# Long convolution on TensorE: whole-array outer stages, 64x64 quarters in the middle, and a new order of the work

## The chip, the core and the metric

The kernel runs on one core of one Trainium2 chip. The metric is the device time of one execution in microseconds. The median of three runs before the change is 393.52 us (393.09 to 393.66).

## The reference

Two layers are computed side by side, both on a sequence of S = 2048 with D = 1024 channels in bf16, and their outputs are concatenated.

Layer A is a long convolution. A filter of four taps is run over `k`, the result is multiplied by `v` to give `kv`, and `kv` is convolved along the sequence with `ssm_k` (one filter of length 2048 for each channel), in the reference by an FFT of length 4096. A skip term is added and the result is multiplied by `q`:

```
kv  = k_shift * v
y_f = rfft(pad(kv)) * rfft(pad(ssm_k))
y   = irfft(y_f)[:S] + kv * ssm_D
a   = q * y
```

Layer B is a diagonal state-space recurrence with 1024 complex states:

```
for t in range(L):
    h = Lam_bar * h + Bu[:, t, :]
y = 2 * real(einsum(h, Cmat)) + x * Dskip
```

## The kernel before

The convolution is a discrete Fourier transform of length 4096 split into two stages of 128 and 32 points, done with matmuls against constant matrices. It has these steps. The name in front is the task's name in the code.

- `kvm`, `kva`, `kvb`, `kvc` (DVE) make `kv` for one residue n2 of the time index modulo 16 (16 residues).
- `hl`, `hT`, `hc` load the filter and transpose it on TensorE (L571), because its time index lies along the free dimension.
- `am` (L548, for `kv`) and `hm` (L590, for the filter) are stage 1: matmuls with 64 rows, one for each half p of the partitions. `ae` and `he` copy the result from PSUM on ACT, `ast` and `hst` store it to DRAM (`Ys_kv`, `Ys_h`), with 2 KB or 1 KB rows.
- `lh`, `lk` load it back regrouped, for pair i of 16 pairs of frequency groups; `lw` loads the pair's constants into one of three slots.
- `sh`, `sk` (L616) are stage 2 for the filter and for `kv`: matmuls with 64 output columns, two of them for one PSUM bank. `she`, `ske` (L624) copy on ACT.
- `pr` (L630) multiplies on DVE all four combinations of real and imaginary half (4096 elements per partition).
- `sa` (L640) is the inverse of stage 2: four matmuls of 64 rows for each output, which add the four products with their signs. `sae` (L647) copies, `vst` stores to DRAM (`Vs`).
- `vl` loads again, `a3` (L668) is the inverse of stage 1 with 64 output columns, `a3e` copies, `qm` multiplies by `q`, `ost` stores.

Layer B goes over 16 chunks of 128 time steps: `U` (L441, 128-column matmuls), `ue` (ACT), `r1`, `r2`, `sc` (the scan), `r3`, `r4` (all DVE), `y` (L485, 512-column matmuls, with the skip term in L490), `ye` (ACT), `yst`. `cy` carries the state from chunk to chunk.

All tasks are written by hand into one long text, `ORDER`, which names every task, its place in SBUF (`a` with a unit number) and its PSUM banks (`p`). Each engine executes its instructions in that order. Loads are issued on the queue of SP, stores on the queue of POOL. An engine that waits holds up all that stands behind it on the same engine.

The change and the steps of the prediction touch `a_constants`, `ORDER` and the tasks `kp`, `vp`, `am`, `hT`, `hm`, `l2`, `s2`, `s2e`, `pr`, `sa`, `sae`, `vl`, `qp`, `a3_`, `ost`.

Of the kernel before, what the change touches and what calls it, by code (L numbers as in the profile page):

```python
# [31 lines left out]
def a_constants():
    n1 = np.arange(64)[:, None]; k1 = np.arange(64)[None, :]
    ang = 2 * np.pi * n1 * (k1 + 0.5) / N1
    F1 = np.concatenate([np.cos(ang), -np.sin(ang)], axis=1)
    F1 = np.concatenate([F1, F1], axis=0)
    G = np.concatenate([np.cos(ang.T), -np.sin(ang.T)], axis=0) * 2 / NFFT
    n2 = np.arange(N2); k2 = np.arange(N2)
    W = np.zeros((128, NPAIR, 640))
    for g in range(NG):  # L40
        i, gs = divmod(g, 2)
        fw = np.zeros((N2, 2, 2, 2, 2, N2))
        wr = np.zeros((2, N2, N2, 2, 2))
        wi = np.zeros((2, N2, N2, 2, 2))
        for l in range(2):
            kk = (32 * l + g) + N1 * k2
            phi = 2 * np.pi * np.outer(n2, kk + 0.5) / NFFT
            cph, sph = np.cos(phi), np.sin(phi)
            fw[:, 0, l, 0, l, :] = cph
            fw[:, 1, l, 0, l, :] = sph  # L50
            fw[:, 0, l, 1, l, :] = -sph
            fw[:, 1, l, 1, l, :] = cph
            wr[l, :, :, 0, l] = cph.T
            wr[l, :, :, 1, l] = sph.T
            wi[l, :, :, 0, l] = -sph.T
            wi[l, :, :, 1, l] = cph.T
        W[:, i, gs * 128:(gs + 1) * 128] = fw.reshape(128, 128)
        rows = slice(64 * gs, 64 * gs + 64)
        W[rows, i, 256:384] = wr.reshape(64, 128)
        W[rows, i, 384:512] = -wr.reshape(64, 128)  # L60
        W[rows, i, 512:640] = wi.reshape(64, 128)
# [9 lines left out]
kvm.1:a36 bT.4.1:p2 bcv.7.1 bT.0.1:p1 bcv.0.1 bc.7.0 bl.4.0:a26 bT.4.0:p5 bT.2.1:p4 bcv.2.1 cl.1.0:a27 cT.1.0:p7 cc.1.0 x.1:a52 bl.1.0:a34
U.1.0.0:a32p0 bT.1.0:p1 bc.1.0 U.1.1.0:p4 U.1.1.1 U.1.3.0:p3 U.1.3.1 bc.4.0 ue.1.1 kva.1 hl.2:a40 bl.5.0:a35 ue.1.3 vp.1.0:a42 stt x.0:a44 z2 z1
U.0.0.0:a46p6 kvb.1:a45 kp.-2.0 U.0.0.1 ue.0.0 bT.5.0:p7 U.0.3.0:p1 U.0.3.1 ue.0.3 U.0.1.0:p5 kp.-2.1 kvm.0:a48 cl.3.1:a29 vp.0.0:a30 bc.5.0 U.0.1.1
vp.0.1 kvc.1 bcv.4.1 cT.3.1:p4 kva.0 cc.3.1 cl.0.0:a28 kp.1.0 am.1.1:p3p2 ae.1.0.1:a34 U.1.0.1 ue.1.0 ae.1.1.1 kp.1.1 U.0.2.0:p6 U.0.2.1 kvm.2:a4
ue.0.2 ue.0.1 x.2:a16 U.2.0.0:a18p1 kvb.0:a17 kva.2 am.1.0:p7p4 ae.1.1.0 ae.1.0.0 cT.0.0:p3 kvc.0 am.0.0:p0p2 am.0.1:p6p5 ae.0.0.1:a26 ast.1 kvb.2:a45
U.1.2.0:p4 ld_sd:a17 ae.0.1.0 hl.0:a36 ae.0.1.1 hl.3:a38 hl.1:a24 hT.0.6:p7 hc.0.6:a20 kvm.3:a48 U.2.0.1 ae.0.0.0 hm.0.6.1:p6p2 he.0.6.1.0:a22
U.2.1.0:p5 he.0.6.1.1 r1.0:a28 hm.0.6.0:p7p0 he.0.6.0.0 he.0.6.0.1 hT.0.1:p6 ue.2.0 cl.2.0:a21 hst.0.6.1 vp.1.1 kvc.2 kva.3 am.2.0:p2p7 cx.6.1 r2.0:h0
ae.2.0.0:a46 cl.1.1:a4 cT.1.1:p0 cc.0.0 U.2.1.1 ue.2.1 kvb.3:a20 cc.1.1 cl.2.1:a5 cl.3.0:a6 kp.2.0 ae.2.1.0 cT.2.1:p1 am.2.1:p2p3 sc.0.1 ae.2.1.1
# [12 lines left out]
hT.1.1:p1 hc.1.1:a42 hst.0.3.0 hst.0.7.1 y.1.1.2 y.1.1.3 vp.4.0:a26 ye.1.0:a43 hc.1.4:a52 ue.3.3 r1.3:a36 ast.4 U.4.1.1 hm.1.1.1:p5p1 he.1.1.1.1:a18
kp.5.0 he.1.1.1.0 hm.1.1.0:p4p2 kvb.7:a42 vp.3.0:a40 vp.3.1 y.2.0.0:p6 ye.1.1 yst.1 ue.4.1 y.2.0.1 hT.1.7:p1 y.2.0.2 he.1.1.0.1 kvc.6 hc.1.7:a34
hm.1.5.0:p5p3 hm.1.5.1:p0p2 he.1.5.1.0:a22 he.1.5.1.1 kp.4.0 he.1.5.0.0 y.2.1.0:p1 kp.4.1 he.1.5.0.1 y.2.1.1 kvc.7 vp.4.1 am.7.0:p0p2 ae.7.0.0:a46
am.7.1:p5p3 kvm.8:a28 ae.7.1.1 ae.7.1.0 kva.8 he.1.1.0.0 kvb.8:a35 ae.7.0.1 hc.1.2:a25 y.2.0.3 y.2.1.2 r2.3:h0 ye.2.0:a40 cy.3 U.4.3.0:p0 kvc.8
U.4.3.1 ue.4.3 y.2.1.3 sc.3.0 am.8.1:p3p2 ye.2.1 yst.2 am.8.0:p4p5 hm.1.2.1:p7p6 hst.1.1.0 hT.1.0:p0 sc.3.1 ast.7 ae.8.1.1:a42 he.1.2.1.1:a28
hT.1.6:p1 hc.1.0:a16 hd.1 hT.1.3:p2 he.1.2.1.0 hm.1.2.0:p6p0 he.1.2.0.0 hst.1.2.0 yst.0 U.4.2.0:p7 hc.1.3:a35 he.1.2.0.1 ae.8.0.1 kp.5.1 hst.1.2.1
U.4.2.1 hm.1.0.1:p6p2 kvm.11:a36 kp.6.0 x.5:a41 U.5.0.0:a6p0 ue.4.2 U.5.0.1 U.5.2.0:p3 ae.8.0.0 he.1.0.1.1:a30 U.5.2.1 lw.1:w1 hc.1.6:a25 he.1.0.1.0
ae.8.1.0 r1.4:a48 hm.0.5.1:p7p4 ue.5.0 he.0.5.1.0:a32 kva.11 hm.1.0.0:p2p1 hm.0.5.0:p6p5 ast.8 hst.1.1.1 he.0.5.0.1 he.1.0.0.0 he.0.5.0.0 he.0.5.1.1
# [645 lines left out]
```

## Time and profile before

| | |
|---|---|
| median of the runs | 393.52 us |
| the profiled execution's own time | 393.14 us |
| its span, first to last instruction | 390.9 us |
| mean granted TensorE clock | 0.988 |
| DMA | 92.41 MB, mean 236 GB/s |
| stage 1 of the convolution (L548, L590) | 37.8 to 183.0 us |
| stage 2 and its inverse (L616, L640) | 182.1 to 319.2 us |
| inverse of stage 1 (L668) | 348.1 to 370.7 us |

The profile is one execution, recorded by the hardware. PE is TensorE's matmuls, PEld its weight loads, DVE VectorE, ACT ScalarE, POOL GpSimd, SP SyncE, which here only issues DMAs. "Busy" is the time in which an engine had an instruction running. In the strip of 40 digits each digit is the busy share of one fortieth of the span in tenths. A shape such as 128\*64 beside a matmul is that of the weights: rows by columns. Matmuls are pipelined: an isolated one lasts some 0.38 us, while in a stream of 512-column ones the next starts after 0.216 us, so costs are taken from the distance between starts.

### The profile page before, as it was taken

What the parts mean: (1) busy time and instruction counts of PE and PEld (TensorE: products, weight loads), DVE (VectorE), ACT (ScalarE), POOL (GpSimd) and SP (SyncE); (2) the same over time, 40 slices, a digit from 0 to 9 for tenths busy, and PEclk for the clock granted to TensorE, in tenths of its full rate; (3) what the DMA queues carried; (4) which work ended last, traced back from release to release, by engine and by line L of the source; (5) the groups of instructions that cost most, each with busy time, mean ns of one, the idle gap of its engine ahead of it and who ended that gap; (6) DMA issues with size and microseconds to landing.
All of it is one profiled execution on the core that took longest, in us unless ns stands there. A gap on an engine that the chain in (4) does not pass through costs nothing.

```text
span 390.9 us, 9198 instructions
## 1 busy us (share of the span) xinstructions
PE 363.6 (93%) x3821; PEld 236.1 (60%) x3849; DVE 320.8 (82%) x257; ACT 277.9 (71%) x530; POOL 67.8 (17%) x111
## 2 busy tenths in 40 slices
PE   4689799999999999999999999996999999999990
PEld 2589689456658577567554547553564549955440
DVE  5768998899989999999999925959369398998950
ACT  4698599985699956628677999795588973158530
POOL 5000112035004430311000020010002011001171
PEclk9999999999999999999999999999999999999996
DMA  6999999999948979677757787699586728998695
GB/s 189 263 272 210 277 282 204 259 314 341 260 110 219 266 242 223 203 242 244 256 203 223 250 284 217 164 202 352 149 231 216 227 121 283 297 245 229 237 267 183
DMA packets 55365, 92.41 MB, mean 236 GB/s; under 512 B 29422, under 2 KB 31502, under 8 KB 55324
## 3 DMA queue, kind: packets, MB, share of 16 engines
q1 hardware_dynamic: 45468, 58.21, 58.4%
q0 software_dynamic: 9856, 33.62, 25.6%
q8 instruction: 30, 0.49, 0.6%
q14 instruction: 11, 0.09, 0.1%
HBM read 51.96 MB, written 33.55 MB: 219 GB/s over the span
## 4 chain that ended last, share of the span: by engine, by line
PE 68%; DMA 12%; ACT 7%; issue 6%; SPq 3%; POOL 1%; DVE 0%; POOLq 0%; ACTq 0%
PE bank L441 24%; PE bank L485 22%; PE bank L616 7%; DMA arena<-in_A_k_dram 6%; PE bank L640 6%; PE bank L571 4%; DMA arena<-in_A_ssm_k_dram 3%; PE bank L590 2%; DMA wslot<-a_c_W 2%; PE bank L548 2%; ACT arena L647 2%; PE bank L490 2%; DMA out_dram<-arena 1%; ACT arena L624 1%; ACT arena L675 1%
## 5 line engine op out<-in xcount | busy, mean ns | idle before, releaser
L485 PE MATMUL bank<-CT,gslot 128*128 128x512 bf16 x484 | 122.3, 381 | 2.2 <-issue 0.9
L441 PEld LDWEIGHTS <-BT 128*128 128x128 bf16 x2048 | 115.7, 98 | 11.9 <-issue 9.4
L441 PE MATMUL bank<-arena,BT 128*128 128x128 bf16 x2048 | 121.9, 219 | 0.2
L485 PEld LDWEIGHTS <-gslot 128*128 128x128 bf16 x512 | 44.1, 98 | 53.2 <-issue 12.7
L469 DVE TENSOR_TENSOR_SCAN gslot<-rtab,gslot 128x1040 bf16<-128x1040 f32 x32 | 72.8, 2311 | 3.6 <-ACT gslot L465 3.1
L624 ACT CAST arena<-bank 128x512 bf16<-128x512 f32 x128 | 67.1, 657 | 10.2 <-PE bank L616 10.1
L630 DVE TENSOR_TENSOR arena<-arena 128x4096 bf16<-128x4096 bf16 x16 | 36.3, 2289 | 30.9 <-ACT arena L624 30.4
L443 ACT CAST arena<-bank 128x512 bf16<-128x512 f32 x64 | 38.7, 618 | 28.4 <-PE bank L441 20.7
L496 ACT CAST arena<-bank 128x512 bf16<-128x512 f32 x32 | 19.4, 606 | 38.3 <-PE bank L485 35.2
L456 DVE TENSOR_TENSOR arena<-arena,Z 128x4096 bf16<-128x4096 bf16 x16 | 36.6, 2287 | 7.5 <-ACT arena L443 3.4
L554 ACT CAST arena<-bank 128x512 bf16<-128x512 f32 x64 | 35.3, 617 | 6.5 <-PE bank L548 6.2
L596 ACT CAST arena<-bank 128x512 bf16<-128x512 f32 x64 | 35.4, 632 | 3.7 <-PE bank L590 3.5
L456 DVE TENSOR_TENSOR arena<-gslot,Z 128x4096 bf16<-128x4096 bf16 x16 | 36.6, 2288 | 0.6
L647 ACT CAST arena<-bank 128x512 bf16<-128x512 f32 x64 | 34.7, 641 | 2.5 <-PE bank L640 2.5
L616 PE MATMUL bank<-arena,wslot 128*64 128x512 bf16 x256 | 32.4, 389 | 3.4 <-DMA wslot<-a_c_W 3.4
L525 DVE TENSOR_TENSOR arena<-arena 128x4096 bf16<-128x4096 bf16 (+3 forms) x16 | 30.0, 1881 | 4.5 <-ACT arena L335 3.2
L599 POOL DMA_DIRECT2D Ys_h<-arena x32 | 23.2, 725 | 38.3 <-ACT arena L596 38.2
L640 PE MATMUL bank<-arena,wslot 64*128 64x512 bf16 x256 | 29.6, 377 | 0.0
L490 PE MATMUL bank<-Dd,arena 128*128 128x128 bf16 x128 | 28.2, 220 | 0.3 <-issue 0.2
L650 POOL DMA_DIRECT2D Vs<-arena x16 | 8.5, 535 | 112.0 <-ACT arena L647 76.5
L557 POOL DMA_DIRECT2D Ys_kv<-arena x16 | 11.6, 727 | 85.7 <-ACT arena L554 83.1
L616 PEld LDWEIGHTS <-wslot 128*64 128x64 bf16 x256 | 13.8, 110 | 19.4 <-issue 5.0
(95 smaller groups left out, 353.9 us busy)
## 6 DMA issues: line engine op xcount, KB each, us to landing
Ys_kv<-arena POOLq DMA_DIRECT2D x16, 512.0 KB, 4.7
Ys_h<-arena POOLq DMA_DIRECT2D x32, 256.0 KB, 3.9
out_dram<-arena POOLq DMA_DIRECT2D x32, 256.0 KB, 6.1
arena<-Ys_h SPq DMA_DIRECT2D x16, 512.0 KB, 5.7
arena<-Ys_kv SPq DMA_DIRECT2D x16, 512.0 KB, 4.9
Vs<-arena POOLq DMA_DIRECT2D x16, 512.0 KB, 5.0
arena<-Vs SPq DMA_DIRECT2D x16, 512.0 KB, 8.3
arena<-in_A_k_dram SPq DMA_DIRECT2D x18, 256.0 KB, 6.9
```

The source lines that it names most:

```text
L441: nc.tensor.matmul(pu[:, w, jl, :], BT[:, 2 * jp + jl, w, d, :], xT[:, d, :], start=(d == 0), stop=(d == ND - 1))
L443: E["ue"] = lambda i, jp: nc.scalar.copy(st["u", i][:, :, 2 * jp:2 * jp + 2, :], st.pop(("pu", i, jp)))
L456: nc.vector.tensor_mul(m, s_, win(Z))
L469: nc.vector.tensor_tensor_scan(gf, rtab[:].rearrange("p j t -> p (j t)"), gf, 0.0, ALU.mult, ALU.add)
L485: nc.tensor.matmul(py, h[:, w, j, 2:GW], CT[:, j, w, dh * 512:(dh + 1) * 512], start=(j == 0 and w == 0), stop=(j == NJ - 1 and w == 1))
L490: nc.tensor.matmul(py[:, dl * P:(dl + 1) * P], st["xT", i][:, d, :], Dd[:, d, :], start=False, stop=False)
L596: nc.scalar.copy(st["yh", hf, s][:, p, e, :], st.pop(("pb", hf, s, e, p)))
L616: nc.tensor.matmul(pt[64 * gs:64 * gs + 64, :], st["w", i][:, gs * 128 + w * 64:gs * 128 + w * 64 + 64], st[nm, i][:, gs, dh * 512:(dh + 1 ...
L624: nc.scalar.copy(st["X", nm, i][:, w, dh * 512:(dh + 1) * 512], st.pop(("ps", nm, i, w, dh)))
L630: nc.vector.tensor_mul(st["P", i], st.pop(("X", "k", i)).unsqueeze(2).to_broadcast([P, 2, 2, D]), st.pop(("X", "h", i)).unsqueeze(1).to_br ...
L640: nc.tensor.matmul(st["pv", i, gs, dh], st["w", i][rows, 256 + m * 128:384 + m * 128], st["P", i][rows, cx, ch, dh * 512:(dh + 1) * 512], ...
L647: nc.scalar.copy(st["vsb", i][:, gs, dh * 512:(dh + 1) * 512], st.pop(("pv", i, gs, dh)))
```

## The change

The Fourier transform is split in another way over the partitions.

- Stage 1 (`am`, `hm`) uses all 128 rows: each half p has its own constants, with zeros in the rows of the other half, so that one matmul of 128 rows takes the place of one with 64 rows. `hT` transposes whole 128-column blocks. `a3` uses 128 output columns and adds the two halves in PSUM.
- Stage 2 and its inverse work in quarters of the array: 64 rows by 64 columns, four independent matmuls for one task, for each of 32 groups g. The two halves of the channels go to the two column halves, the two frequencies l of a group to the two row halves.
- The product takes two combinations instead of four: the spectrum of the filter is kept twice, as it is and with its 32-partition quadrants exchanged (`sw`, four DMAs from SBUF to SBUF for each pair, issued on POOL). `pr` still covers 4096 elements per partition, in place.
- The scratch tensors in DRAM have another order of rows: stage 2 reads and writes runs of 2 KB where it had 4 KB. Loads of `k`, `v`, `q` and the store of the output cover all 128 partitions in one DMA instead of two.
- The constants of a pair grow from 640 to 704 columns. `ORDER` is written anew. `sj`, `sje`, `swp` are defined and not used in it.

```diff
-    F1t = const.tile([P, P], BF16, name="F1t")
-    Gt = const.tile([P, 64], BF16, name="Gt")
+    F1t = const.tile([P, 2, P], BF16, name="F1t")
+    Gt = const.tile([P, 2, P], BF16, name="Gt")
...
     def am(n2, dh):
-        src = st["kv", n2]
         for p in range(2):
             st["pa", n2, p, dh] = bank()
-        for p in range(2):
-            rows = slice(64 * p, 64 * p + 64)
-            nc.tensor.matmul(st["pa", n2, p, dh], F1t[rows, :], src[rows, dh * 512:(dh + 1) * 512], start=True, stop=True)
+            nc.tensor.matmul(st["pa", n2, p, dh], F1t[:, p, :], st["kv", n2][:, dh * 512:(dh + 1) * 512], start=True, stop=True)
...
-                hv = st["hk", 4 * hf + c].rearrange("q (n p s) -> q s p n", p=2, s=16)
-                for p in range(2):
-                    nc.tensor.transpose(pt[64 * p:64 * p + 64, e, c, :], hv[:, 2 * s + e, p, :], ident[:])
+                hv = st["hk", 4 * hf + c].rearrange("q (m s) -> q s m", s=16)
+                nc.tensor.transpose(pt[:, e, c, :], hv[:, 2 * s + e, :], ident[:])
...
+    def s2(nm, g, c0=0):
+        i, a = divmod(g, 2)
+        pk = "j" if c0 else nm
+        for l in range(2):
+            st["ps", pk, g, l] = bank()
+        for dh in range(2):
+            for l in range(2):
+                rows = slice(64 * l, 64 * l + 64)
+                nc.tensor.matmul(st["ps", pk, g, l][64 * dh:64 * dh + 64, :], st["w", i][rows, a * WC + c0:a * WC + c0 + 64],
+                                 st[nm, i][rows, a, dh * 512:(dh + 1) * 512], start=True, stop=True)
...
+    def swap(dma, i, q):
+        o = q ^ 1
+        dma(st["hab", i][32 * q:32 * q + 32, 1, :, :, :], st["hab", i][32 * o:32 * o + 32, 0, :, :, :])
+    E["sw"] = lambda i, q: swap(gpd, i, q)
...
     def pr(i):
+        hab = st["hab", i].rearrange("p t a l d -> p t (a l d)")
+        nc.vector.tensor_mul(hab, st.pop(("x16", i)).rearrange("p a l d -> p (a l d)").unsqueeze(1).to_broadcast([P, 2, 2 * D]), hab)
...
+    def sa(g):
+        i, a = divmod(g, 2)
+        for dh in range(2):
+            st["pv", g, dh] = bank()
+        for t in range(2):
+            for l in range(2):
+                for dh in range(2):
+                    rows = slice(64 * dh, 64 * dh + 64)
+                    c0 = a * WC + 96 + 128 * l + 64 * t
+                    nc.tensor.matmul(st["pv", g, dh][64 * l:64 * l + 64, :], st["w", i][rows, c0:c0 + 64],
+                                     st["hab", i][rows, t, a, l, :], start=(t == 0), stop=(t == 1))
...
     def a3_(n2, dh):
         pt = bank()
         st["po", n2, dh] = pt
         for p in range(2):
-            nc.tensor.matmul(pt[64 * p:64 * p + 64, :], Gt[:], st["vv", n2][:, p, dh * 512:(dh + 1) * 512], start=True, stop=True)
+            nc.tensor.matmul(pt, Gt[:, p, :], st["vv", n2][:, p, dh * 512:(dh + 1) * 512], start=(p == 0), stop=(p == 1))
```

A stretch of the new `ORDER` in the middle stage, for the places of `sw`, `pr` and `sa`:

```
sae.19.1 sw.11.0 pr.11 sk.20:p2p0 lh.12:a16
...
y.10.0.1 sae.22.0 U.12.2.1 y.10.0.2 sae.23.0 sw.10.3 pr.10
```

More of the change, by code (lines that the diff above doesn't have):

```diff
@@ L28 @@
 UNIT = 1024
+WC = 352
 GW = 130
 def a_constants():
[L33 to L37, printed above, removed]
+    g = np.arange(NG)[:, None, None]; l = np.arange(2)[None, :, None]; cc = np.arange(2)[None, None, :]
+    k1 = (2 * g + l + 0 * cc).reshape(-1); cs = (cc + 0 * g + 0 * l).reshape(-1)
+    m = np.arange(128)
+    ang = 2 * np.pi * (m // 2)[:, None] * (k1 + 0.5)[None, :] / N1
+    tr = np.where(cs[None, :] == 0, np.cos(ang), -np.sin(ang))
+    F1 = np.stack([tr * (m % 2 == p)[:, None] for p in range(2)], axis=1)
+    G = np.stack([tr.T * (m % 2 == p)[None, :] * 2 / NFFT for p in range(2)], axis=1)
@@ L38, in a_constants @@
     n2 = np.arange(N2); k2 = np.arange(N2)
-    W = np.zeros((128, NPAIR, 640))
+    W = np.zeros((2, 64, NG, WC))
     for g in range(NG):
[L41 to L44, printed above, removed]
         for l in range(2):
-            kk = (32 * l + g) + N1 * k2
+            kk = (2 * g + l) + N1 * k2
             phi = 2 * np.pi * np.outer(n2, kk + 0.5) / NFFT
             cph, sph = np.cos(phi), np.sin(phi)
[L49 to L61, printed above, removed]
+            fw = np.zeros((2, N2, 2, N2))
+            fw[0, :, 0, :] = cph
+            fw[1, :, 0, :] = sph
+            fw[0, :, 1, :] = -sph
+            fw[1, :, 1, :] = cph
+            W[l, :, g, 0:64] = fw.reshape(64, 64)
+            W[l, :, g, 64:96] = fw[:, :, 0, :].reshape(64, 32)
+            wa = np.zeros((2, N2, 2, N2)); wb = np.zeros((2, N2, 2, N2))
+            for w, sg in ((0, 1.0), (1, -1.0)):
+                wa[w, :, 0, :] = sg * cph.T
+                wa[w, :, 1, :] = sg * sph.T
+                wb[w, :, 0, :] = -sph.T
+                wb[w, :, 1, :] = cph.T
+            for dh in range(2):
+                W[dh, :, g, 96 + 128 * l:160 + 128 * l] = wa.reshape(64, 64)
+                W[dh, :, g, 160 + 128 * l:224 + 128 * l] = wb.reshape(64, 64)
@@ L71 @@
[L71 to L78, printed above, removed]
@@ L91 @@
[L91 to L98, printed above, removed]
@@ L135 @@
-ske.10.0.0 sk.10.0.1:p1 qp.3.0:a36 U.11.3.0:p5 U.11.3.1 sc.9.1 ske.10.0.1 she.10.1.0 sae.9.0.1 lw.7:w0 she.10.0.0 ue.11.3 lw.12:w2 sk.12.1.1:p7
-sk.10.1.1:p4 sh.12.1.0:p1 sc.9.0 ske.10.1.1 ske.12.1.1:a38 r3.9:a40 she.12.1.0:a20 sh.10.0.1:p0 sk.12.0.1:p3 sh.7.0.0:p6 she.10.0.1 sh.7.1.1:p5
-lh.11:a48 she.7.1.1:a50 r4.9 y.9.1.0:p4 y.9.1.1 y.9.1.2 yst.8 vst.5 ske.12.0.1 she.7.0.0 pr.10:a4 ue.10.2 lk.7:a16 sk.7.1.0:p7 ske.7.1.0:a2 x.13:a52
-sk.7.0.1:p1 ske.7.0.1 sh.12.0.1:p0 sk.7.1.1:p5 sh.7.1.0:p3 she.7.1.0 qp.2.0:a40 sk.7.0.0:p6 ske.7.0.0 lk.8:a42 ske.7.1.1 sh.7.0.1:p2 lh.13:a18
@@ L147 @@
-sk.14.1.1:p4 ske.14.1.1:a12 she.8.0.0 sh.14.0.1:p3 she.14.0.1 sh.14.1.0:p2 she.14.1.0 sk.14.1.0:p1 ske.14.1.0 pr.8:a8 cy.11 lh.15:a42 y.10.1.2
-y.10.1.3 sa.13.1:p5p4 sae.13.0.1:a44 sa.13.0:p0p3 sae.13.1.0 sae.13.1.1 ye.10.1:a32 sa.8.0:p2p1 sae.13.0.0 sa.8.1:p5p3 sae.8.1.1:a30 sae.8.1.0
-y.10.0.0:p4 vst.13 vst.10 lw.15:w0 qp.5.0:a0 ld_G yst.9 sae.8.0.1 sae.8.0.0 vst.8 ue.12.0 y.10.0.1 y.10.0.2 y.10.0.3 ye.10.0 sh.15.1.1:p6
-she.15.1.1:a2 sc.11.0 sk.15.1.1:p0 sk.15.0.0:p3 ske.15.0.0:a24 ske.15.1.1 sc.11.1 lw.11:w1 sk.11.1.1:p1 sh.11.0.0:p5 sh.15.1.0:p2 she.15.1.0
@@ new lines @@
+sae.7.1:a36 sae.6.0 she.10.0 sae.6.1 U.10.2.0:p5 U.10.2.1 U.11.3.0:p7 U.11.3.1 she.11.0 sae.7.0 lh.9:a18 ue.10.2 lw.6:w0 she.11.1 sk.10:p2p3 ue.11.3
+ske.10.1:a12 sh.12:p6p1 ske.10.0 she.12.0:a0 she.12.1 sh.13:p0p5 she.13.0 sk.11:p4p7 yst.4 y.8.1.0:p3 y.8.1.1 y.8.1.2 yst.7 y.8.1.3 she.13.1
+sk.13:p2p6 ske.11.0 pr.4 sa.9:p1p0 x.12:a38 sa.8:p5p4 r1.9:a24 ske.11.1 ye.8.1:a7 vst.3 sae.9.1:a34 sk.12:p7p3 sae.9.0 y.8.0.0:p0 sae.8.1 y.8.0.1
+y.8.0.2 ske.12.0:a14 ske.12.1 ske.13.1 sae.8.0 ske.13.0 r2.9:h0 cy.9 y.8.0.3 ye.8.0 lk.7:a30 lw.8:w2 sh.17:p1p4 she.17.0:a24 she.17.1 sh.16:p7p3
@@ new lines @@
+sc.10.0 sae.14.1 sc.10.1 sk.23:p2p3 y.9.1.0:p1 sw.9.3 y.9.1.1 y.9.1.2 ske.23.1:a32 ske.23.0 sae.15.1 r2.11:h2 y.9.1.3 sk.22:p5p6 ye.9.1 ske.22.0 pr.9
+lh.10:a24 lw.10:w1 sh.21:p7p4 she.21.1:a12 she.21.0 lh.13:a26 sh.20:p3p2 she.20.0 U.12.1.0:p0 ske.22.1 U.12.1.1 she.20.1 ue.12.1 sk.21:p1p5 r3.10:a44
+r4.10 ske.21.1:a36 sa.19:p4p7 ske.21.0 sa.18:p3p6 sae.18.1:a28 yst.5 vst.8 sw.11.1 sw.11.2 sw.11.3 sae.19.1 sw.11.0 pr.11 sk.20:p2p0 lh.12:a16
+ske.20.1 vst.7 cy.11 y.10.1.0:p5 y.10.1.1 sae.18.0 ske.20.0 y.10.1.2 sc.11.1 sae.19.0 y.10.1.3 sc.11.0 r3.11:a44 ye.10.1:a20 lw.13:w0 sh.26:p1p6
@@ new lines @@
+she.31.0 she.31.1 sw.15.3 sw.15.0 sw.15.1 sw.15.2 r3.12:a12 r4.12 sk.31:p6p1 U.13.3.0:p7 ske.31.1:a10 ske.31.0 U.13.1.0:p0 U.13.3.1 U.13.1.1
+sa.24:p2p3 sk.30:p5p1 ue.15.0 pr.14 ue.13.1 sa.25:p6p4 U.13.2.0:p0 U.13.2.1 qp.7:a32 sae.24.0:a36 U.15.3.0:p2 U.15.3.1 qp.3:a28 ue.13.3 sae.25.1 yst.6
+U.15.2.0:p7 sae.25.0 qp.2:a24 sa.28:p4p6 ske.30.1 sae.24.1 vst.12 ske.30.0 ue.13.2 qp.4:a30 pr.15 ue.15.3 sa.29:p1p3 sa.30:p5p0 qp.0:a26 sae.28.1:a18
+sae.28.0 x.14:a39 sa.31:p2p6 y.12.0.0:p4 y.12.0.1 y.12.0.2 U.15.2.1 y.12.0.3 sae.29.0 sae.29.1 U.14.0.0:a22p1 U.14.3.0:p3 U.14.3.1 vst.14 sae.30.0:a10
@@ L224, in full_kernel @@
     gslots = [const.tile([P, 2, NJ, GW], BF16, name="gslot%d" % s) for s in range(NGS)]
-    wslots = [const.tile([P, 640], BF16, name="wslot%d" % s) for s in range(NWS)]
+    wslots = [const.tile([P, 2 * WC], BF16, name="wslot%d" % s) for s in range(NWS)]
     arena = const.tile([P, NUNITS * UNIT], BF16, name="arena")
@@ L584, in hm @@
     def hm(hf, s, e):
-        src = st["hT", hf, s]
         for p in range(2):
             st["pb", hf, s, e, p] = bank()
-        for p in range(2):
-            rows = slice(64 * p, 64 * p + 64)
-            nc.tensor.matmul(st["pb", hf, s, e, p], F1t[rows, :], src[rows, e, :], start=True, stop=True)
+            nc.tensor.matmul(st["pb", hf, s, e, p], F1t[:, p, :], st["hT", hf, s][:, e, :], start=True, stop=True)
     E["hm"] = hm
@@ L607, in l2 @@
         st[nm, i] = sb(2).rearrange("p (g d) -> p g d", g=2)
-        spd(st[nm, i], Ys.rearrange("n (c l g) d -> (n c l) g d", c=2, l=2)[:, 2 * i:2 * i + 2, :])
+        spd(st[nm, i], Ys.rearrange("(g r) d -> r g d", r=P)[:, 2 * i:2 * i + 2, :])
     E["lh"] = lambda i: l2("h", Ys_h, i)
     E["lk"] = lambda i: l2("k", Ys_kv, i)
-    def s2(nm, i, w, dh):
-        pt = bank()
-        st["ps", nm, i, w, dh] = pt
-        for gs in range(2):
-            nc.tensor.matmul(pt[64 * gs:64 * gs + 64, :], st["w", i][:, gs * 128 + w * 64:gs * 128 + w * 64 + 64],
-                             st[nm, i][:, gs, dh * 512:(dh + 1) * 512], start=True, stop=True)
@@ new lines, in full_kernel, with she, ske @@
+    E["sh"] = lambda g: s2("h", g)
+    E["sk"] = lambda g: s2("k", g)
+    E["sj"] = lambda g: s2("h", g, 32)
+    def she(nm, t, g, l):
+        i, a = divmod(g, 2)
+        if ("hab", i) not in st:
+            st["hab", i] = sb(4).rearrange("p (t a l d) -> p t a l d", t=2, a=2, l=2)
+        nc.scalar.copy(st["hab", i][:, t, a, l, :], st.pop(("ps", nm, g, l)))
+    E["she"] = lambda g, l: she("h", 0, g, l)
+    E["sje"] = lambda g, l: she("j", 1, g, l)
+    def ske(g, l):
+        i, a = divmod(g, 2)
+        if ("x16", i) not in st:
+            st["x16", i] = sb(2).rearrange("p (a l d) -> p a l d", a=2, l=2)
+        nc.scalar.copy(st["x16", i][:, a, l, :], st.pop(("ps", "k", g, l)))
@@ L632, in full_kernel @@
     E["pr"] = pr
-    def sa(i, dh):
-        for gs in range(2):
-            st["pv", i, gs, dh] = bank()
-        for n, (cx, ch, m) in enumerate(((0, 0, 0), (1, 1, 1), (0, 1, 2), (1, 0, 2))):
-            for gs in range(2):
-                rows = slice(64 * gs, 64 * gs + 64)
-                nc.tensor.matmul(st["pv", i, gs, dh], st["w", i][rows, 256 + m * 128:384 + m * 128],
-                                 st["P", i][rows, cx, ch, dh * 512:(dh + 1) * 512], start=(n == 0), stop=(n == 3))
+    def sa(g):
+        i, a = divmod(g, 2)
+        for dh in range(2):
+            st["pv", g, dh] = bank()
+        for t in range(2):
+            for l in range(2):
+                for dh in range(2):
+                    rows = slice(64 * dh, 64 * dh + 64)
+                    c0 = a * WC + 96 + 128 * l + 64 * t
+                    nc.tensor.matmul(st["pv", g, dh][64 * l:64 * l + 64, :], st["w", i][rows, c0:c0 + 64],
+                                     st["hab", i][rows, t, a, l, :], start=(t == 0), stop=(t == 1))
@@ L656, in full_kernel, with qp @@
     E["vl"] = vl
[L658 to L661 removed]
+    def qp(r):
+        st["qt", r] = sb(2).rearrange("p (s d) -> p s d", s=2)
+        spd(st["qt", r], qr[:, 2 * r:2 * r + 2, :])
     E["qp"] = qp
```

227 lines of the change are left out of this document (108 added, 119 removed).

## The prediction

> **What bounds the kernel now.** I read the page first: which engine is full, and where in time.
>
> ```profile
> span 390.9 us, 9198 instructions
> PE 363.6 (93%) x3821; PEld 236.1 (60%) x3849; DVE 320.8 (82%) x257; ACT 277.9 (71%) x530; POOL 67.8 (17%) x111
> ...
> PE   4689799999999999999999999996999999999990
> ...
> DVE  5768998899989999999999925959369398998950
> ACT  4698599985699956628677999795588973158530
> ```
>
> PE is full from the second slice to the last but one, apart from one dip. DVE is as full as PE in the first half only. The table by windows (PE, PEld, DVE, ACT and POOL busy time, clock, DMA share, GB/s) puts numbers to this:
>
> ```profile
> 0.00:20.00 20.00, 11.73 (x77) 7.63 (x78) 12.75 (x45) 11.98 (x19) 4.97 (x13) 1.00 0.87 225
> 80.00:100.00 20.00, 19.73 (x204) 12.55 (x205) 20.00 (x16) 12.56 (x25) 8.68 (x12) 1.00 1.02 320
> 260.00:280.00 20.00, 16.38 (x143) 8.71 (x142) 14.90 (x8) 12.19 (x25) 0.28 (x1) 0.91 0.90 257
> 300.00:320.00 20.00, 19.72 (x182) 10.57 (x183) 13.34 (x8) 17.18 (x35) 2.91 (x6) 1.00 0.59 187
> 380.00:390.90 10.90, 1.83 (x9) 0.63 (x7) 0.00 (x0) 1.17 (x2) 1.75 (x3) 0.72 0.62 200
> ```
>
> So the span is PE's queue, plus 8.3 us idle at the start, one wait of 3.4 us near 264 us, and about 9 us after PE's end near 381.8 (last store). Only PE's queue and what holds it up can move the end. The chain of waits, in order of time, prices PE's work: start, duration, line, count.
>
> ```profile
> 95.81 1.93 PE bank L571 x32
> ...
> 204.37 1.94 PE bank L485 x9
> 206.31 3.56 PE bank L640 x32
> ...
> 264.75 7.05 DMA wslot<-a_c_W
> ...
> 280.11 2.06 PE bank L616 x18
> ...
> 322.95 14.29 PE bank L441 x256
> ```
>
> A full 512-column matmul costs 1.94/9 = 0.216 us, a 128-column one 14.29/256 = 0.056. Stage 2 (L616, `sh`/`sk`) costs 2.06/9 = 0.229 per pair of half-width matmuls: both run at once. The inverse (L640, `sa`) costs about 0.217 per pair (3.56/16 less a change of shape). A half-width transpose of `hT` costs 1.93/32 = 0.060, more than a whole one: two 64-column weight loads take 0.12 us while the streams need 0.056, so such a load costs 0.060.
>
> A change of array shape has a price too, in the timeline of PE:
>
> ```profile
> 345.20 2.97 PE L485 MATMUL bank<-CT,gslot 128*128 128x512 bf16 x13
> 348.10 2.13 PE L668 MATMUL bank<-arena,Gt 128*64 128x512 bf16 x18
> 350.17 1.96 PE L441 MATMUL bank<-arena,BT 128*128 128x128 bf16 x32
> ```
>
> Thirteen at 0.216 put the next start at 348.01; it came at 348.10, and the way back loses as much: 0.1 us per change. Counted in ORDER, the kernel changes shape 160 times, the new one 57 times.
>
> **The change on PE.**
> - `hT`: 256 half transposes to 128 whole: 256 x 0.060 - 128 x 0.056 = 8.2 saved.
> - `am`, `hm`: 64 pairs at 0.22 become 128 whole matmuls at 0.216: 13.6 added.
> - `a3`: 32 pairs become 64 whole: 6.8 added.
> - `sh`, `sk`: 128 pairs at 0.229 (29.3) become 64 groups of four quarters.
> - `sa`: 128 pairs at 0.217 (27.8) become 64 groups of four.
> - Changes of shape: 103 fewer x 0.1: 10 saved.
>
> No row shows a group of four quarters. From below it costs the 0.216 of its columns; from above 0.446, the two kinds of pair one after another. I take 0.240: rows of before run two row halves at once and two column halves at once, and four loads of 64 columns at 0.060 set the pace. So 128 groups cost 30.7, saving 26.4. PE's sum: -8.2 + 13.6 + 6.8 - 26.4 - 10 = -24 us.
>
> **Where that lies.** The end needs `r4.6` (DVE) and then all of PE's queue from `y.6` on. Before, `r4.6` ends at 190.06 with DVE idle 17.7 until then, 12 of it in the first 40 us; `y.6` starts 0.7 later. In the new order DVE's queue up to `r4.6` holds the same work and one `r1` more (2.29). PE's front part gets about 8.5 shorter, but DVE sets the front: that saving is lost. The front moves +2.3; bounds -6 (DVE's 5.9 us of idle between 40 and 190 us go) and +8 (a start with less cover).
>
> From `y.6` on, counting ORDER: before, 118 pairs of `sh`/`sk` (27.0), 128 of `sa` (27.8), 32 of `a3` (7.0), 55 changes (5.4): 67.2. After, 58 groups (13.9), 64 groups (15.4), 64 whole `a3` (13.8), 48 changes (4.7) and four `U` tasks more (3.6): 51.4. The rest (80 `y` parts, 50 `U` tasks) is the same. So -15.8 of some 185.6.
>
> **The rest.** ACT's copies (128 in stage 2, 64 after `sa`, 64 in `a3`), the product `pr` (2.29 each) and the scans stay: DVE's 321 and ACT's 278 us lie beside PE. From the first `sh` to the last `sa` ACT has about 124 us, PE 121: if a copy is late, PE has no cover left there. Whole instead of half loads (`kp`, `vp`, `qp`) save SP some 26 issues of 0.45 us, off the path; `lw` grows from 160 to 176 KB, nothing while it comes ahead. Spectrum reads in 2 KB instead of 4 KB runs: nearest row is the read of Vs, already in 2 KB runs, 8.3 us to landing against 5.7 and 4.9; 0 to 3 us, hidden as loads are issued ahead.
>
> New are 64 `sw` DMAs, SBUF to SBUF, 128 KB each, on POOL. Issuing costs 0.54 to 0.73 (rows of POOL): about 40 us on a queue 17% busy. They wait for ACT's copies `she`; behind them wait `vst` and `yst`, whose readers come much later. Each `pr` waits for four landings, `sa` for `pr`, and PE's queue for `sa`. No row has this transfer; nearest is the 256 KB store of Ys_h, 3.9 us. I take 3 to 4, mostly issued ahead of need: nothing per pair; a new transfer can't gain anything, and at worst each pair waits for its last issue (0.6) and a landing 1.3 later than in quiet (2.6 at the quietest store, 3.9 median), 1.9 us. [...] The middle stage moves about 42 MB instead of 31 (137 us, 222 GB/s before), so some 320 GB/s, as in the fullest window above. So I add one more wait like that for wslot: 3.4.
>
> **Sum.** `r4.6` at 192.4, `y.6` at 193.1. Before, PE took 191.1 from 190.76 to 381.83, 5.5 over the counted work. After: 169.8 + 5.5 + 3.4 = 178.7, PE ends at 371.8; 9.1 for the tail: span 380.9. The profiled execution took 393.14, 2.24 over its span: 383 us. The median of the runs is 0.4 higher, which changes nothing.
>
> **Rivals.**
> 1. *More is gained.* The front loses idle (-6), groups cost 0.216 (-2.9), no extra wait (-3.4): 371 us. For it: DVE's queue meets its `kvm` work earlier. Against: all three must come together.
> 2. *Slower: the exchange comes late.* Nine of the sixteen `pr` stand directly behind their last `sw` in ORDER. If PE waits 0.9 us per pair on average, 16 x 0.9 = 14.4 eats the gain; that is the point. At the bound of 1.9 it is 30 on top of 379.6 (the sum without the extra wait): 410; at half of that, 395. For it: 320 GB/s. Against: POOL can run ahead, `she` is done long before `pr`.
> 3. *Slower: quarters run two at a time.* 122 groups from `y.6` on at 0.446: + 25, 408 us. Against: pairs of both kinds overlap today.
> 4. *Weights do not load beside the other quarter of their row half.* Each group then shows two loads, 0.12: 122 x 0.12 = 14.6, 398 us. The L616 row speaks against it: both its loads serve all rows, and the pair still takes 0.229. [...]
> 5. *It does nothing at the end*: the front moves by its bound of 8 instead of 2.3 (+5.7) and the extra wait comes twice (+3.4): 392 us.
>
> **Chances.** Forecast (376 to 390) 0.48; rival 1, 0.20; rival 2, 0.17; rival 3, 0.06; rival 4, 0.03; rival 5, 0.06. About 0.2% (0.8 us) is what a measurement can tell from no change. Faster: 0.48 + 0.20 + 0.03 of the mild ends of rivals 2 and 5 = 0.71; same: 0.03 of rival 5; slower: the rest of rivals 2 to 5, 0.26. The range runs from 369 to 403: it takes in rival 1, rival 4 and the milder half of rival 2.
>
> **What would show it.** Right: PE busy near 340; L616 and L640's successors with 64*64 shapes, 256 each, in groups of 0.24; `hT` 128 at 0.056; `r4.6` near 192 us; DVE's share over 84%. Wrong: `pr` or `sa` waiting for a DMA from arena to arena; groups near 0.45; PE idle over 35 us; `r4.6` later than 200.

## The result, and the profile after

The changed kernel takes 375.9 us (median of 4 runs, 375.68 to 381.63) beside 393.59 us for the kernel before on the same chip: a ratio of 0.953, 95% interval 0.946 to 0.960. A second series gave 377.65 beside 395.01, 0.961 (0.953 to 0.968). Where one number is wanted below, it is the mean of the two, 0.957, which is 17 us of 394. Every ratio is to runs of the kernel before on the same chip. A run more than 1.5% over the fastest of its kernel counts in the medians and not in the ratios, and the profiled execution of the first series was such a run (381.63 us), so all rows of after are from that of the second: 377.37 us, span 375.6.

The page after, the answer to the page of before:

```profile
span 375.6 us, 9054 instructions
PE 345.2 (92%) x3721; PEld 231.6 (62%) x3721; DVE 319.8 (85%) x257; ACT 276.6 (74%) x530; POOL 98.1 (26%) x167
PE   5689999999999999999999799969999987999990
DVE  5999999999999999999895497949996569698950
```

PE has 18.4 us less to do and is still the fullest engine. Two things are new. DVE is full from its second slice on, where before it showed 7, 6, 8. And PE, full before but for one dip, has three dips between 206 and 320 us. The table by windows (columns as before) says the same; the first row is the kernel before, the others are after:

```profile
20.00:40.00 20.00, 19.07 (x290) 18.47 (x289) 15.19 (x27) 18.22 (x35) 0.00 (x0) 1.00 1.14 244
```

```profile
0.00:20.00 20.00, 11.62 (x73) 7.30 (x73) 15.40 (x46) 12.23 (x21) 4.90 (x13) 1.00 0.82 255
20.00:40.00 20.00, 19.04 (x264) 17.86 (x265) 20.00 (x33) 18.78 (x34) 0.51 (x1) 1.00 1.03 319
...
260.00:280.00 20.00, 19.40 (x198) 10.63 (x200) 19.20 (x11) 16.87 (x35) 8.12 (x15) 1.00 0.99 282
300.00:320.00 20.00, 15.70 (x199) 10.66 (x197) 15.70 (x9) 10.46 (x22) 6.69 (x12) 0.91 0.98 250
360.00:375.60 15.60, 6.70 (x37) 3.02 (x34) 3.50 (x3) 2.96 (x6) 2.74 (x4) 0.87 0.46 176
```

In the first 40 us DVE is busy 35.4 us instead of 27.9 (12.75 + 15.19 before): 7.5 us of its idle time are gone. At 300 to 320 us the DMA engines are busy 98% of the time instead of 59%, and PE lost 4.3 us and part of its clock there. The chain of waits (start, duration, what) names the cause of two of the dips:

```profile
46.47 0.50 PE bank L558 x8
...
205.77 5.64 DMA arena<-arena
211.59 2.30 DVE arena L633
213.93 1.32 PE bank L645 x16
...
301.27 8.89 DMA arena<-arena
310.29 2.30 DVE arena L633
312.63 1.06 PE bank L645 x16
```

The exchange (`sw`) lands 5.6 and 8.9 us after its issue, the product `pr` (L633) waits for it, and PE's inverse (L645, `sa`) for `pr`. The table of waits adds them up (engine and line, waited for: us in total, times, longest):

```profile
DVE arena L633 <- DMA arena<-arena: 20.3, 7, 9.2
...
PE bank L645 <- DVE arena L633: 10.6, 4, 4.3
```

The groups of four quarters, of which before had no row, are in the timeline of PE (start, length, line, form, count):

```profile
284.49 0.84 PE L604 MATMUL bank<-arena,wslot 64*64 64x512 bf16 x12
285.27 0.39 PE L479 MATMUL bank<-CT,gslot 128*128 128x512 bf16 x1
...
287.56 1.03 PE L645 MATMUL bank<-arena,wslot 64*64 64x512 bf16 x16
288.53 1.69 PE L479 MATMUL bank<-CT,gslot 128*128 128x512 bf16 x7
```

Twelve quarters and a change of shape take 0.78 us, sixteen and a change 0.97. Less 0.1 for the change, a group of four costs 0.227 and 0.218. Over the whole trace a group starts 0.216 or 0.240 us after the one before it, in the mean 0.229 for `sh` and `sk` and 0.219 for `sa`: 1 to 6% more than one whole matmul (0.216).

In the table below "back" is the time from the end of `r4.6` to PE's end. "Idle" is PE's idle time in it, "clock" what the granted clock took: one minus the clock, times the window, over windows of 4 us. "Work" is the rest, so PE's work at full clock (us, one profiled execution each). The three runs below that have no row here are judged by their times alone.

| kernel | span | `r4.6` ends | DVE idle until then | back | idle | clock | work |
|---|---|---|---|---|---|---|---|
| before | 390.9 | 190.1 | 17.7 | 191.7 | 5.0 | 1.7 | 185.0 |
| after | 375.6 | 178.5 | 4.7 | 188.2 | 12.1 | 5.1 | 171.0 |
| no exchange | 362.9 | 179.1 | 5.4 | 178.3 | 4.7 | 3.4 | 170.2 |
| outer stages alone | 393.1 | 186.1 | 14.0 | 200.6 | 5.8 | 1.7 | 193.1 |
| half transposes | 386.8 | 187.5 | 13.5 | 190.4 | 13.5 | 6.8 | 170.1 |
| half loads | 380.5 | 185.3 | 11.2 | 186.3 | 12.9 | 1.7 | 171.7 |
| q late | 368.8 | 178.5 | 4.7 | 181.4 | 7.7 | 3.4 | 170.3 |
| more q late | 369.8 | 179.5 | 5.6 | 181.4 | 9.6 | 0.0 | 171.8 |

The total came out near the forecast, but not by its steps: the front gave 11.6 us where a loss of 2.3 was forecast, and the back 3.5 where a gain of 12.4 was. The experiments had two questions: what sets the front, and where the back's gain went.

### The profile page after: what moved, and what is told of

Same layout as the page of the kernel before. It is cut to its first block, busy times and chain, and to the rows that moved or that the text cites. A ratio compares the mean times of both kernels' runs of the same rounds, so it can differ in the third digit from the quotient of the medians.

```text
span 379.9 us, 9024 instructions
## 1 busy us (share of the span) xinstructions
PE 343.3 (90%) x3691; PEld 230.5 (61%) x3721; DVE 319.4 (84%) x257; ACT 276.5 (73%) x530; POOL 98.1 (26%) x167
## 4 chain that ended last, share of the span: by engine, by line
PE 39%; DVE 28%; DMA 16%; issue 8%; ACT 3%; POOL 2%; SPq 1%; DVEq 0%; POOLq 0%; ACTq 0%
PE bank L479 13%; PE bank L435 13%; DMA arena<-arena 6%; DVE gslot L463 6%; DVE arena L516 6%; DVE arena L450 4%; PE bank L673 3%; DMA arena<-Ys_h 3%; DMA Vs<-arena 3%; DVE arena L523 2%; DVE arena L633 2%; PE bank L645 2%; DMA arena<-in_A_k_dram 2%; PE bank L574 2%; POOL arena L627 2%
## 5 line engine op out<-in xcount | busy, mean ns | idle before, releaser
L479 PE MATMUL bank<-CT,gslot 128*128 128x512 bf16 x489 | 127.1, 387 | 1.8 <-issue 0.4
L435 PEld LDWEIGHTS <-BT 128*128 128x128 bf16 x2048 | 117.6, 98 | 10.5 <-issue 4.3
L479 PEld LDWEIGHTS <-gslot 128*128 128x128 bf16 x512 | 45.9, 99 | 52.0 <-issue 7.2
L633 DVE TENSOR_TENSOR arena<-arena 128x4096 bf16<-128x4096 bf16 x16 | 36.6, 2287 | 28.9 <-DMA arena<-arena 16.0
L437 ACT CAST arena<-bank 128x512 bf16<-128x512 f32 x64 | 39.0, 626 | 23.5 <-PE bank L435 22.4
L653 ACT CAST arena<-bank 128x512 bf16<-128x512 f32 x64 | 35.9, 632 | 15.3 <-PE bank L645 11.2
L627 POOL DMA_DIRECT2D arena<-arena x64 | 31.2, 495 | 47.6 <-ACT arena L614 45.5
L542 ACT CAST arena<-bank 128x512 bf16<-128x512 f32 x64 | 35.9, 622 | 7.8 <-PE bank L536 7.7
L580 ACT CAST arena<-bank 128x512 bf16<-128x512 f32 x64 | 36.0, 632 | 5.9 <-PE bank L574 5.0
L622 ACT CAST arena<-bank 128x512 bf16<-128x512 f32 x64 | 36.9, 666 | 1.9 <-PE bank L604 1.7
L614 ACT CAST arena<-bank 128x512 bf16<-128x512 f32 x64 | 34.6, 641 | 2.4 <-PE bank L604 1.3
L490 ACT CAST arena<-bank 128x512 bf16<-128x512 f32 x32 | 19.0, 602 | 23.4 <-PE bank L479 20.3
L645 PE MATMUL bank<-arena,wslot 64*64 64x512 bf16 x256 | 18.7, 410 | 14.3 <-DVE arena L633 14.2
L656 POOL DMA_DIRECT2D Vs<-arena x16 | 11.9, 746 | 56.3 <-ACT arena L653 47.5
L395 PE MATMUL bank<-ident,arena 128*128 128x128 bf16 x192 | 18.7, 273 | 4.6 <-DMA arena<-in_B_B_im_dram 2.8
```

The costliest lines, as they stand in the source:

```text
L435: nc.tensor.matmul(pu[:, w, jl, :], BT[:, 2 * jp + jl, w, d, :], xT[:, d, :], start=(d == 0), stop=(d == ND - 1))
L437: E["ue"] = lambda i, jp: nc.scalar.copy(st["u", i][:, :, 2 * jp:2 * jp + 2, :], st.pop(("pu", i, jp)))
L479: nc.tensor.matmul(py, h[:, w, j, 2:GW], CT[:, j, w, dh * 512:(dh + 1) * 512], start=(j == 0 and w == 0), stop=(j == NJ - 1 and w == 1))
L542: nc.scalar.copy(st["ysb", n2][:, p, dh * 512:(dh + 1) * 512], st.pop(("pa", n2, p, dh)))
L580: nc.scalar.copy(st["yh", hf, s][:, p, e, :], st.pop(("pb", hf, s, e, p)))
L622: nc.scalar.copy(st["x16", i][:, a, l, :], st.pop(("ps", "k", g, l)))
```

## Experiments on the back: the exchange

**The same again**, for a second profile.

> The changed kernel as it is, for a second profile. Theory (the front gave the gain, the back gave its own saving away): r4.6 ends at 178 to 179 us again, 11 to 12 us ahead of before, with DVE idle under 6 us until then; from there to PE's end it takes 184 to 188 us, where before took 191, and PE idles 6 to 12 us in the middle stage, mostly ahead of the inverse matmuls. Time 375 to 376. Rival (the waits belong to the one profiled execution alone): PE idle under 4 us in the middle stage.

Measured: 377.65 us, 0.961 (0.953 to 0.968), 2 us over the expected time. `r4.6` ends at 178.5 and PE idles 12.1 us behind it, so the waits were not those of one execution alone.

**No exchange.** `sw` leaves ORDER, all 64 of it, and both products and both inverse matmuls read the half that is there (`h0`; `x_` is the spectrum of `kv`), so the kernel leaves the exchanged half's product out of the result:

```
-sw.0.1 ... sw.15.2
...
-        hab = st["hab", i].rearrange("p t a l d -> p t (a l d)")
-        nc.vector.tensor_mul(hab, st.pop(("x16", i))... .to_broadcast([P, 2, 2 * D]), hab)
+        nc.vector.tensor_mul(h0, x_, h0)
+        nc.vector.tensor_mul(x_, x_, h0)
-                                     st["hab", i][rows, t, a, l, :], ...
+                                     st["hab", i][rows, 0, a, l, :], ...
```

> The exchange is left out: no sw transfers, both products and both inverse matmuls use the unexchanged half, in two DVE instructions of 2048 elements in place of one of 4096 (0.15 us longer per pair). Theory (PE waits for the exchange in the middle stage): 6 to 11 us less, 365 to 370, and DVE no longer waits for a DMA from arena to arena. Rival (these waits only stand where weights, copies or the stores of the inverse would end late anyway): within 2 us of the changed kernel, 374 to 378.

Measured: 363.84 us, 0.922 (0.916 to 0.929). The exchange costs 0.035 of 394, some 14 us, more than the 6 to 11 expected. PE's work is the same (170.2 against 171.0), and the idle time falls from 12.1 to 4.7, about what it was before the change (5.0). So the loss is in waits, not in the quarters.

This run leaves out one thing more. Its inverse needs only the first of the two products, which takes 1.22 us, where after needs one of 2.29. At after's four waits of PE for `pr` that can be up to 4.3 of the 14 us. No run separates it, and it is in every figure below that sets a kernel with the exchange against one without.

**The exchange's traffic without its wait.** As above, but the 64 transfers are issued, from a constant tile into the half that nobody reads:

```
-        dma(st["hab", i][32 * q:32 * q + 32, 1, :, :, :], st["hab", i][32 * o:32 * o + 32, 0, :, :, :])
+        dma(st["hab", i][32 * q:32 * q + 32, 1, ...]..., BT[32 * o:32 * o + 32, ...]...[:, 0:2048])
```

> As the run without the exchange, but the 64 transfers are still issued, from a constant tile into the unused half: same bytes, same issue places, no wait of the product for them. Theory A (the wait itself costs): as fast as without them, within 2 us. Theory B (the 8.4 MB more on loaded DMA engines make weights, spectra and stores late): as slow as the changed kernel, 374 to 377.

Measured: 373.0 us, 0.939 (0.930 to 0.948), between the two theories. The ratio rests on two of the four runs, 371.84 and 367.64 us; all four would give 0.944. Against no exchange 0.939 is 0.0165 more, 6.5 us for the traffic and its issues, though no product waits for them (9 us by the medians). The rest, some 7 us (0.957 less 0.939; 4 us by the medians), is the wait with the later start of the inverse. The intervals are wide enough for 3 to 10 us each. All four runs (367.64 to 375.56) lie below every run of after (375.68 to 381.63) and above every run of no exchange (360.58 to 364.81): that both parts are there is shown, their shares are not.

**Loads of q behind the reads of Vs.** In the kernel after, five loads of q of 512 KB stand together in SP's queue between 289 and 301 us. The timeline of the queue (start, length, line, count) shows it; the length includes a wait of SP of 7.8 us behind the second load, and the last three go out at 297.7, 299.2 and 300.4 us; the second fence is the same place with `qp.3`, `qp.0`, `qp.2` and `qp.4` moved behind `vl.7`, `vl.0`, `vl.5` and `vl.8`:

```profile
289.07 11.69 SPq L666 DMA_DIRECT2D arena<-in_A_q_dram  x5
```

```profile
288.26 0.38 SPq L665 DMA_DIRECT2D arena<-in_A_q_dram  x1
```

```
-... U.15.3.1 qp.3:a28 ue.13.3 ... sae.25.0 qp.2:a24 sa.28:p4p6 ... ue.13.2 qp.4:a30 pr.15 ... sa.30:p5p0 qp.0:a26
+... vl.7:a10 qp.3:a28 ... vl.5:a2 qp.2:a24 ... vl.0:a12 qp.0:a26 ... vl.8:a46 qp.4:a30
```

> The changed kernel with four loads of q (2 MB) moved on SP's queue from ahead of the last products to behind loads of Vs. In the profile of the changed kernel three of these land at the same time as the last exchange, which takes 9 to 13 us. Theory (these loads stand in the exchange's way): the last exchange lands in 5 to 6 us and the time is 2 to 4 us less. Rival (the loads of Vs, needed next, pay for it, or the waits are elsewhere): within 1 us, or slower.

Measured: 370.45 us beside 394.4, 0.940 (0.936 to 0.944): 6 to 7 us faster than after, more than the 2 to 4 expected, and faster than both kernels. The wait at 312.6 us is gone, and the last four transfers of the exchange land in 2.6 to 2.8 us. A load of `x`, which stood behind the loads of q in SP's queue (300.8 us), has also left that stretch (288.7); the run does not tell its part from theirs. The waits:

```profile
DVE arena L632 <- DMA arena<-arena: 14.9, 4, 8.0
...
PE bank L644 <- DVE arena L632: 5.9, 3, 3.9
```

**Two more loads of q late** (`qp.1` behind `vl.13`, `qp.6` behind `vl.12`):

```
-... lk.10:a10 qp.1:a8 sae.17.0 ... vst.11 qp.6:a34 sw.13.3
+... vl.13:a0 qp.1:a8 a3.13.1 ... vl.12:a6 qp.6:a34 a3.12.1
```

> All of the four moved loads of q as in the run before, and two more: `qp.1` (which stood beside the wait at 248 us) and `qp.6` go behind `vl.13` and `vl.12`; only `qp.5` and `qp.7` stay. Theory (the loads of q stand in the way of the exchange and of the reads for the middle stage): part of the 7.0 us that PE still idles in the back goes, 366 to 370 us median, against 370.5 with four moved. Rival (what is left is the exchange's own traffic and order): the same 370 within 2 us. Rival (six loads at the end crowd the reads of Vs before `a3`): slower, 372 to 376, with PE idle before L672's matmuls after 320 us.

Measured: 372.16 us beside 393.8, 0.946 (0.940 to 0.951), not told apart from four moved. The wait at 248 us becomes shorter (3.86 to 2.94 us), but PE now waits for reads of Vs at 343 to 350 us (0.6, 1.2 and 1.2 us), so the rival of crowding at the end is partly true too.

**Loads of q late, and no exchange.**

The two edits above, four loads of q moved and `sw` left out, in one kernel.

> The exchange is left out (both products and both inverse matmuls read the half that is there, as in the earlier run without it), with the four loads of q late. Theory (loads of q hurt because they delay the exchange): without the exchange the move brings nothing more, so 361 to 365 us as without the exchange before (363.8), and the exchange still costs 6 to 8 us beside the late loads of q, of the 13.8 that it cost beside the early ones. Rival (loads of q delay the reads of the spectra and weights just as much): another 3 to 6 us go here too, 357 to 361.

Measured: 364.06 us, 0.921 (0.916 to 0.927), the same as no exchange alone (0.922), within some 3 us. Without the exchange the place of the loads of q is worth nothing that these runs can tell; so in the main they cost time by delaying the exchange, not the spectra or the weights. The exchange still costs 0.940 less 0.921, 7 us, of the 14.

## Experiments on the front

**The outer stages alone.** The kernel before, with its order, and only `hT`, `am`, `hm` (like `am`, not shown) and `a3` on the whole array, with the constants for it:

```
-            rows = slice(64 * p, 64 * p + 64)
-            nc.tensor.matmul(st["pa", n2, p, dh], F1t[rows, :], src[rows, ...], start=True, stop=True)
+            nc.tensor.matmul(st["pa", n2, p, dh], F1t[:, p, :], src[:, ...], start=True, stop=True)
...
-                for p in range(2):
-                    nc.tensor.transpose(pt[64 * p:64 * p + 64, e, c, :], hv[:, 2 * s + e, p, :], ident[:])
+                nc.tensor.transpose(pt[:, e, c, :], hv[:, 2 * s + e, :], ident[:])
...
-            nc.tensor.matmul(pt[64 * p:64 * p + 64, :], Gt[:], st["vv", n2][:, p, ...], start=True, stop=True)
+            nc.tensor.matmul(pt, Gt[:, p, :], st["vv", n2][:, p, ...], start=(p == 0), stop=(p == 1))
```

> The kernel before, with its own order, and only the outer stages on the whole array (hT, am, hm, a3). PE's sum: -8.2 (hT) +13.6 (am, hm) +6.8 (a3) -10.2 (changes of shape, 160 to 58) = +2; from y.6 on +6.8 -0.8 = +6, ahead of it -4. Theory (the front is set by DVE): the front does not get shorter, +6, so 398 to 401. Rival (the front is set by PE): +2, so 394 to 397.

Measured: 394.04 us over 10 runs, 0.9995 (0.9955 to 1.0034): nothing, nearer to the rival's +2 than to the theory's +6. Two parts cancel. `r4.6` comes 4.0 us earlier (and DVE's idle time falls by 3.7), so PE's saving in the front is not lost as I had it; and the back has 8.1 us more work, 6.8 of which are `a3`'s by the count. The outer stages alone are a trade of front against back, and what pays is the middle stage in quarters.

**Half transposes in the new kernel.** `hm` gets other constants for them, and the unused columns in a pair's constants go (704 to 640):

```
-                nc.tensor.transpose(pt[:, e, c, :], hv[:, 2 * s + e, :], ident[:])
+                for p in range(2):
+                    nc.tensor.transpose(pt[64 * p:64 * p + 64, e, c, :], hv[:, 2 * s + e, p, :], ident[:])
```

> The changed kernel, but the filter is again transposed in 256 half transposes (128x64) and only hm gets other constants for it. That puts 8.2 us and some 3 us of changes of shape back on PE, all of it ahead of y.6. Theory (in the new order DVE alone sets the front): r4.6 stays within 2 us of 178.5 and the time within 3 us of the changed kernel. Rival (PE sets the front there too): r4.6 at 186 to 190, and 8 to 11 us slower.

Measured: 385.43 us, 0.978 (0.973 to 0.983), 8 us slower than after. `r4.6` moves by 9.0, and DVE idles 8.8 us longer, 6.4 of it in one wait at 166 us for the scan's input. The back's work is unchanged. 7.4 us of transposes and some changes of shape thus go into the end in full: PE's work ahead of `r4.6` sets the front too.

**Loads of k and v later.** Six reads of B go ahead of `kp.-2`, so that SP reaches `kp` and `vp` that much later:

```
-... wbe.4 kp.-2 bcv.7.1 ...
+... wbe.4 bl.0.1 bl.6.1 bl.6.0 bl.5.1 bl.3.1 bl.5.0 kp.-2 bcv.7.1 ...
```

> The changed kernel with one edit in its order: the first three loads of k wait on SP's queue behind six more loads of B (1.5 MB, some 5 us at 290 GB/s), so that DVE's first kvm starts at about 22 instead of 17 us. Theory (the front's gain is DVE's early start): r4.6 and the end come 3 to 5 us later. Rival (DVE's queue has slack later on): under 1 us.

Measured: 382.71 us, 0.970 (0.965 to 0.975), some 5 us slower than after, by the time alone. The new order's early loads of k and v are thus needed for its gain.

**Loads in halves.**

```
-            spd(t_, kr[:, 2 * r:2 * r + 2, :])
+            for h in range(2):
+                spd(t_[64 * h:64 * h + 64, :, :], kr[64 * h:64 * h + 64, 2 * r:2 * r + 2, :])
```

(the same for `vp` and `qp`)

> The changed kernel with the loads of k, v and q in two DMAs of 64 partitions again. Theory (SP's issues are off the path): within 1 us. Rival (26 issues of 0.45 us on SP delay the first loads): r4.6 1 to 3 us later and the time as much.

Measured: 383.7 us, 0.973 (0.969 to 0.977), 6 to 7 us slower, more than either expected, with `r4.6` 6.8 us later. DVE idles 6.5 us more: 2.3 ahead of its first product, which starts at 20.1 us instead of 17.8, and 4.2 in two waits for the scan's input, at 85 and 164 us. So the whole loads stood on the path; whether by their fewer issues or by earlier landings the run does not tell.

The three costs (9.0 by half transposes, about 5 by late loads, 6.8 by halves) add up to more than the 11.6 that the front gained. They are no shares of it: in the new kernel DVE idles only 4.7 us until `r4.6`, so anything that delays PE or the loads there is late next.

## Why the prediction was right in its sum and wrong in two of its steps

The two steps are "DVE sets the front: that saving is lost" and "nothing per pair" for the exchange. One left out a gain and the other a loss, and that they nearly cancelled is luck.

- **The front, forecast +2.3 us, measured -11.6.** The failed step is "DVE sets the front: that saving is lost". DVE's queue held 172.3 us of work until `r4.6` before and 173.8 after, so it is about as long as I said. But of its 17.7 us of idle the table of waits puts 6.6 down to ACT, 4.9 to PE and 2.3 to loads of `k` and `v`, and I took the 12 us in the first 40 as fixed and only 5.9 (5.7 by the trace) as movable (the bound of -6). Nearly all could go: 4.7 are left. PE's saving counts, as 4.0 us with the outer stages alone and 9.0 lost with half transposes show; how the 11.6 divide among PE, loads and order is not shown.
- **Whole loads, forecast nothing.** "Some 26 issues of 0.45 us, off the path" failed: 6.8 us. I took them for covered; 2.3 us show at the start and 4.2 in two later waits.
- **PE's work in the back, forecast -15.8, measured -14.0.** The traces have 58 changes of shape for the 57 counted, at about 0.1 us as taken, and a group of four costs 0.219 to 0.229 in the mean instead of 0.240. By that the back should have saved some 2 us more, not 1.8 less; where these 4 us went is not traced. In the front `hT` costs 0.062 (0.50/8) instead of 0.056, so that it saved 7.4 of the 8.2.
- **Waits in the back, forecast one of 3.4, measured 7.1 more idle and 3.4 more of clock.** The term "I take 3 to 4, mostly issued ahead of need: nothing per pair" was mis-sized: the median landing is 6.0 us, with up to 10.1 and 2.5 for the quietest one in after. By the no-exchange run that term is up to 14 us, 0.9 per pair. This is rival 2, the exchange that comes late, to the point where by its own sum it would have eaten the gain; the front's gain, which I had not counted, paid for it. Against it I had set that POOL can run ahead. It waited 46.0 us in all for ACT's copies `she` (L614) ahead of `sw`; the issues were cheaper than forecast, 0.49 us for 0.54 to 0.73. Two readings behind that term were off as well. Seven, not nine, of the `pr` stand directly behind their last `sw`, two more with one task between. And 31 MB with the exchange's 8.4 make 39, not 42; the stage moved 276 GB/s (180 to 320 us), not 320, with its DMA engines 95% busy all the same.
- **Clock, forecast nothing.** My extra wait had a price for the idle time only. Two windows in the waits' wake (columns as before; the granted clock is 0.57 and 0.69):

```profile
214.50:218.50 4.00, 4.00 (x48) 3.32 (x40) 3.90 (x2) 3.08 (x7) 0.00 (x0) 0.57 0.57 175
...
314.50:318.50 4.00, 4.00 (x22) 1.97 (x21) 3.86 (x4) 1.00 (x3) 2.85 (x5) 0.69 0.61 237
```

Each of after's three dips of the clock took 1.7 us, as the one of before did behind its wait for `wslot`: 3.41 us at a clock of 0.50, from 272.15 to 275.56. A wait of 2.2 us before 213.9 was followed by a dip, and one of 2.9 us in "more q late" by none (its clock is 1.00 in all windows behind `r4.6`), so the length of one wait alone did not decide it here. The traces of before and of after's execution of 381.63 us show more. In each of the two, all changes of the granted clock lie whole multiples of 3.413 us apart (1 and 32 of them in before; 2, 17, 3 and 16 in after). Divided at these points, from the first record (26.39 and 24.71 us) to PE's last matmul, the stretch at full clock ahead of each of the three halvings has 3.11 us (before), 2.14 and 2.36 us (after) of PE's idle time, and one that another at full clock followed has 1.93 us at the most. So in these two the idle time of a stretch tells which waits cost clock; by the lengths above, a short wait cost more (2.2 and 1.7 of clock) than a long one (2.9).
- **The tail** is 8.9 us (9.1 forecast), and the profiled execution lies 1.8 us over its span (2.2).
- **Rivals 3 and 4** are refuted by the groups of 0.216 to 0.240: no two at a time (0.45), and no weight loads of 0.12 in the open.
- **Rival 1** ("more is gained", 371 us) had its first two parts come true, or nearly: the front gained 11.6 against its 6, and two groups in three cost 0.216. The third, no extra wait, did not, and that q late came to 370.45 does not make it so: 2.7 us of idle and 1.7 of clock more than before are still there. Its sum takes -6 as a difference from the forecast, where rival 5 takes +8 as a place; taken like that, rival 1 comes to 368.5.

In the sum: -11.6 in the front, -3.5 in the back and -0.2 in the tail make -15.3 of span, where -10.0 was forecast. Two errors of some 14 and 9 us with opposite signs left 5.6 (377.4 for 383). The first series' median, 375.9, lies at the lower edge of the 376 to 390 that the forecast's chance was given for.

Open is how the 7 us that the exchange still costs with late loads of q divide among its traffic, its waits and the longer product; and why the wait at 248 us outlasts the move of `qp.1` beside it.

## What to carry to other kernels

An engine's idle time before a dependency says that something else sets that stretch; before calling a saving there lost, ask what each of those waits ends on, the first 40 us included. A transfer that stands between two stages is priced by landings under the load of its own stage (here 6.0 us in the median, 2.5 for the quietest), and large loads that are wanted much later belong behind it in the queues (6 to 7 us here). A wait of TensorE cost its length and, here, up to 3.4 us of clock more (q late, behind its wait at 248 us; 1.7 for each dip of after; none in "more q late").

## What the hardware showed that was not expected

- Four 64x64 quarters run at once: a group of four, each with its own weight load (0.105 us), follows a group after 0.216 or 0.240 us, so a quarter takes 0.054 or 0.060 us of the array, beside 0.216 for a whole matmul.
- A transfer of 128 KB from SBUF to SBUF landed in 2.6 to 2.8 us at q late's last exchange (DMA engines 77%, then 32% busy), in 6.0 (median) in after (95% busy), and in 8.9 at after's last exchange, beside loads of 512 KB issued at 297.7, 299.2 and 300.4 us.
- Traffic that no product waits for still cost some 6.5 us of 394 (3 to 10 by the intervals). Between 180 and 320 us the DMA engines are 95% busy in after and 70% without the exchange.
- In before and in after's execution of 381.63 us the granted clock changed at whole multiples of 3.413 us. Up to PE's last matmul, the stretches ahead of its three halvings have 2.14 to 3.11 us of PE's idle time in sum, all others at full clock 1.93 at the most.
